# A fused attention and two mixture layers in one launch: a new hand-written order of all steps, and another buffer pair for two chunks

## The chip, the cores and the metric

The kernel runs on one core of a Trainium2 chip. The metric is the device time of one launch in microseconds (us). A core has TensorE for matmuls and transposes (PE in the profile, with its weight loads listed apart as PEld), VectorE (DVE), ScalarE (ACT), GpSimd (POOL), and SyncE (SP), which here only issues DMA transfers. Each engine runs its own instruction list in order; semaphores tie the lists together.

## The reference, cut to what matters

```
scores = q @ k.T / 8                         # 2 batches, 8 heads, 576 positions, 64 wide
scores[outside a window of 32] = -1e9        # heads 4 to 7: window of 128, every 4th key
attn   = softmax(scores);  x = attn @ v      # x: 1152 tokens x 512

h   = x @ w_in                               # 512 x 1024, w_in and w_out are float64
s   = h * softmax(h)
ln  = (s - mean(s)) / sqrt(var(s) + 1e-6) * g_ln
x   = ln @ w_out                             # 1024 x 512

p   = domain_probs / sum(domain_probs)
out = sum over 4 experts of p[:, e] * (relu(x @ w1[e]) @ w2[e])
```

All of it is float32 in accuracy: a matmul is made of three (hi x hi, hi x lo, lo x hi), so each operand is first split into a rounded hi and a lo = x - hi.

## The kernel before

**Attention** is cut into 12 units, UP.t.b and UD.t.b (P: plain heads, D: dilated heads; t = 0 to 2, b = batch). Each unit is a chain of steps, one instruction or a small group each: mask and scores on PE (L266, L275), max (L296), subtract (L298), exp (ACT L301), sum (L303), reciprocal (L305), normalise (L307), three PE transposes (L326) and a copy of them, product with v (PE L337), and the split of the result into `xhi` (L176) and `xlo` (L250). For five late units the transposes are done by a DVE block transpose and a bounce through DRAM (`da`, read back as `pt<-da`, L320).

**Weights.** `w_in` comes as float64 in four row blocks (`draw0` to `draw3`; block 0 in two halves, steps VI.0 and VI.4, the others VI.1 to VI.3) and is turned into hi and lo on the chip: low word and high word (ACT L190, L192), shift, or (DVE L194, L196), add (L198), hi (a cast, L176), lo (L225). `w_out` is converted likewise in the steps VO.j.t. The loads are lI.j and lO.j.t; lP, lD, lvp and lvd load the attention's operands, in place.

**First mixture layer.** H.t (t = 0 to 8, 128 tokens each) is x @ w_in (PE L367) in quarters or halves over the four row blocks of w_in; H.0:k and H.1:k below are quarter k, which needs the hi and lo of block k. Then come max, exp, s and a scaled difference. T.t transposes that into a buffer pair `hh`, `hl` that holds a chunk of three token tiles (chunk 0: T.0 to T.2, chunk 1: T.3 to T.5, chunk 2: T.6 to T.8); T.3 to T.8 go through DRAM (`dt`, `et`). X.c.dp is the product of chunk c with w_out (PE L444), copied into `xf`.

**Second mixture layer.** Each expert half g has an up product by Strassen's scheme, seven products of half the size (u.0 and u.1 for the two token halves, PE L568, with sums L585 to L617 on ACT, DVE and POOL), and a down product d.t (PE L640, summed into `xf` by L643 and L645). Its operands are prepared in small steps that add and split: WP.g for w1, WV.g for w2 (L483 loads it into `wl6`, `wl7`; a cast makes `wh4`, `wh5`; a subtraction makes the lo), XQ.s for x.

**Order.** A text table `ORDER` names 542 steps; the program walks through it and emits the next step of the named chain each time, so the table alone sets the order of instructions on every engine up to the first down products. A `+` behind a name changes the engine of that step where there is a choice: copies from ACT to DVE, `pick` from DVE to POOL, `poolv` from POOL to DVE. Steps F.n emit n warm-up matmuls (L86) whose results nobody reads. Behind the table a fixed loop emits the rest of the second layer, the same in both kernels.

**Buffers.** `hpools[0]` and `hpools[1]` hold one `hh`, `hl` pair each.

Of the kernel before, what the change touches and what calls it, by code (L numbers as in the profile page):

```python
# [30 lines left out]
ORDER = """
lP.0.0+ lI.4 VI.4+ F.1 F.3 UP.0.0 VI.4 UP.0.0+ F.4 lD.0.0 UP.0.0 VI.4 VI.4 UP.0.0 UD.0.0 UP.0.0+ VI.4+ lD.1.0+ UD.0.0 F.1 UD.0.0+ lP.1.0+ UP.0.0+ lI.0 lP.2.0
lD.2.0+ UD.1.0 UP.1.0 UD.1.0 UD.1.0+ VI.4 UD.0.0+ lI.1+ UP.1.0 UD.0.0 VI.0 lI.2+ UP.0.0+ UP.0.0 F.1 VI.0 UD.1.0+ UP.1.0+ VI.0+ lvp.0.0+ UP.0.0 VI.4+ F.10 VI.0
UD.1.0 UD.0.0 UP.2.0 UP.1.0+ UP.1.0+ UD.1.0+ UD.2.0+ UD.1.0 UP.2.0 VI.0+ UP.2.0+ UP.2.0 VI.1+ UD.0.0+ lvd.1.0+ VI.1+ VI.0+ VI.2+ VI.0+ VI.2 UP.1.0+ lI.3 UD.2.0
lvp.1.0 UD.1.0 UP.2.0+ UD.2.0 UP.1.0 UD.1.0+ UD.0.0 UD.2.0 F.3 VI.1+ UP.0.0 VI.1 UP.2.0+ UP.0.0 VI.1 UP.0.0+ UD.0.0 VI.2 VI.1 F.3 lvd.0.0 UP.1.0 UD.1.0+ UP.1.0
lD.1.1+ UD.1.0 UP.2.0+ VI.1 H.0+ VI.3 UP.1.0 lO.0.0+ misc+ VI.2+ UP.1.0 UD.1.0+ UD.1.1 VI.3+ lO.0.1 lD.0.1+ UD.2.0+ UP.1.0 VO.0.0 UD.1.1 lvd.2.0+ VI.3 VI.2+
UD.1.1+ UD.0.0+ VI.3 lvp.0.1 lP.0.1 lvd.2.1 UD.1.1 H.1 VI.2 UD.2.0 UD.0.0 VI.3 lD.2.1 UD.0.0 VO.0.1 VI.2 UD.2.0+ UD.1.1 VI.3 H.0+ H.1 UD.2.0 UD.1.1 lvp.2.0+
UD.0.1 UD.2.0 VO.0.1+ UP.0.1 VI.3+ UD.0.1 UP.0.1 lP.2.1 UD.0.1+ UP.0.1+ H.0 H.0 UP.2.0 VO.0.0 VO.0.0 UD.2.0 VO.0.1+ UD.0.1 lP.1.1+ UP.2.0 VO.0.0 VO.0.0+ VO.0.1+
UD.2.0 H.0+ UD.2.0 H.0+ UP.2.1+ VO.0.1+ lO.1.1+ UP.2.1+ UD.1.1+ endE+ VO.0.1+ UD.0.1+ H.1 UP.0.1+ UP.2.1+ lvd.0.1+ lvd.1.1 H.1 VO.0.1+ UD.0.1+ H.0 UD.2.1
UD.2.1+ H.1+ UP.2.0 H.2 UP.0.1 VO.1.1+ UD.0.1+ UP.0.1 UD.0.1+ VO.0.0+ UP.2.0 UD.2.1 H.1+ VO.0.0+ VO.1.1 lO.1.0+ H.2+ VO.1.1+ VO.1.1+ UD.2.1+ H.0+ UP.0.1+ UP.2.1  # L40
UP.0.1 UP.0.1 UP.2.0 UP.2.1 UP.1.1+ VO.1.0+ UD.2.1+ UD.0.1 VO.1.1+ H.1+ VO.1.1+ UD.1.1+ lO.2.1+ T.0 UP.1.1+ UD.2.1+ VO.1.0 T.0+ VO.1.0+ UP.1.1 H.3+ H.2+ UD.1.1
T.0 UD.0.1+ UP.0.1 H.3+ VO.1.0 UP.2.1+ VO.1.0+ T.0+ H.2+ UP.1.1+ UD.1.1 UD.2.1+ UD.0.1 H.2 UP.1.1 H.1+ UP.0.1 VO.2.1+ H.2+ UP.0.1+ UD.1.1 UD.2.1+ lO.2.0+ UD.0.1
UP.1.1 H.3+ VO.2.0 UD.1.1 VO.1.0 UP.2.1+ VO.1.1 UD.0.1+ VO.2.1+ UD.1.1 UD.2.1+ VO.1.0+ H.4+ H.3 T.1+ VO.2.1+ UP.2.1 VO.2.1+ lvp.1.1+ H.3+ VO.2.0 T.1+ T.2 T.1
VO.2.0+ H.5+ VO.2.0+ UD.2.1+ UP.2.1 T.2 T.2 H.4 H.5+ UP.1.1+ lvp.2.1+ UP.1.1+ T.1+ VO.2.0+ H.4 lO.3.0 UD.2.1+ T.2 VO.2.0+ UP.1.1+ H.4 VO.2.1 VO.2.1+ VO.3.0
UP.2.1 UD.2.1 VO.2.0 VO.3.0+ lO.3.1 H.5+ H.5+ UD.2.1 X.0.1+ VO.2.1+ UP.1.1+ VO.3.0 H.4+ VO.3.1 H.5+ VO.3.1 H.5+ H.3 UP.2.1 UP.1.1+ X.0.0 VO.3.0+ UP.1.1 VO.3.1+
VO.3.0 endA VO.3.1 UP.2.1+ T.3+ T.3+ VO.3.1+ VO.3.0 VO.3.1 VO.3.0+ VO.3.1 T.4 T.4+ X.0.1+ X.0.1 UP.1.1 UP.2.1+ T.3+ T.3+ X.0.0+ T.5+ X.0.0+ H.6+ T.4 T.3 H.6+
T.3 T.5+ T.5 H.8 T.4+ H.6 T.5+ T.4 H.6+ H.6 T.6 H.7+ H.8 T.6 H.8 T.4+ H.8+ T.5 H.8+ T.8+ H.7 H.7 T.6 T.6 H.7 T.5+ T.8+ T.6 H.7 X.1.0 X.1.0+ X.1.1 T.7+ T.7+ T.7+
T.8+ T.6+ X.1.0 T.8+ X.1.1+ sc endH T.8 X.1.1 T.7 XQ.0 XQ.0+ T.8 T.7+ T.7 X.2.0 XQ.0+ XQ.0 lW.0 XQ.0+ WP.0+ WP.0 XQ.0 WP.0 X.2.0 XQ.0+ WP.0 XQ.0 WP.0+ WP.0+
WP.0 WP.0 WP.0+ XQ.0+ XQ.0 X.2.1+ WP.0 XQ.0 WP.0+ WP.0+ WP.0 XQ.0 WP.0 XQ.0 XQ.0+ XQ.1 u.0+ XQ.0+ X.2.1 WP.0 u.0 lV.0+ endX XQ.1 XQ.1 u.0+ XQ.0 XQ.1 u.0 WV.0
XQ.1 WP.0+ u.0 u.0+ u.0 XQ.1 WP.0 u.0 u.0 lW.1 WP.0 u.0 u.0+ XQ.1 lW.2 WV.0 XQ.1 WV.0 WP.1+ u.1+ u.1 u.0 u.0+ u.0 u.0 u.0 WV.0 XQ.1+ u.0 u.0+ u.0 u.0+ u.0+ u.0  # L50
u.1+ u.0+ u.1 u.1+ XQ.1+ u.0+ u.1 u.1+ u.1 d.0 u.1+ XQ.1+ d.0+ WP.1 u.1 d.3+ XQ.1+ WP.1 d.3 XQ.1 XQ.1+ d.1+ WP.1+ WP.1 d.1 u.1+ u.1+ d.2 WP.1+ lV.1 WP.1 u.1+
u.1+ u.1 WP.1 WP.1 WP.1 u.1+ XQ.1 WP.1 d.2 WP.1 WP.1 u.1 XQ.1+ u.1 u.1 u.1+ WP.1+ WP.1 u.1 WP.1+ u.1 u.1+ u.1 WP.1 WP.1+
"""
# [758 lines left out]
```

## Time and profile before

| | |
|---|---|
| time, three runs | 525.57, 527.25, 528.87 us (median 527.25) |
| the profiled execution's own time | 526.15 us |
| its span in the trace | 524.4 us (1.75 us lie around it) |
| PE busy | 511.9 us, 98% of the span |
| DVE, ACT, POOL busy | 353.0, 191.5, 195.2 us |
| moved by DMA | 46.44 MB, 39.34 MB of it read |

The trace is one execution, 1.1 us below the median of the runs. A row of a timeline gives start, duration, engine, line, operation, the output and input tiles, and in brackets how long the engine had been idle before and what released it. Matmul rows are joined where they follow each other; a matmul's end is modelled, so rows overlap a little.

### The profile page before, as it was taken

The numbers are of one execution on the slowest core, as the hardware profiler recorded it, in microseconds if no ns is written. First come the engines' busy times: TensorE is split into PE (matmuls) and PEld (weight loads), VectorE is DVE, ScalarE is ACT, GpSimd is POOL, SyncE is SP. The second block draws the span as 40 slices with busy tenths as digits, with TensorE's granted clock in tenths as the row PEclk, the third lists the DMA queues.
The fourth block names the chain that finished last, engine by engine and source line by source line (L and its number), as shares of the span: only waits on it lengthen the run. The fifth ranks groups of instructions, "written<-read, shape, count | busy, mean of one in ns | idle before, by whom it ended". The sixth has DMA issues, their size and how long they took to land.

```text
span 524.4 us, 9407 instructions
## 1 busy us (share of the span) xinstructions
PE 511.9 (98%) x3966; PEld 457.8 (87%) x3971; DVE 353.0 (67%) x468; ACT 191.5 (37%) x296; POOL 195.2 (37%) x135
## 2 busy tenths in 40 slices
...
GB/s 326 406 322 159 178 158 71 153 162 201 53 202 67 1 1 87 75 1 1 160 1 1 40 121 0 1 161 1 2 0 162 1 0 81 0 1 1 1 81 100
DMA packets 24490, 46.44 MB, mean 89 GB/s; under 512 B 4480, under 2 KB 9088, under 8 KB 24064
## 3 DMA queue, kind: packets, MB, share of 16 engines
...
HBM read 39.34 MB, written 6.49 MB: 87 GB/s over the span
## 4 chain that ended last, share of the span: by engine, by line
PE 90%; DVE 4%; ACT 3%; DMA 2%; issue 1%; SPq 0%; DVEq 0%; ACTq 0%
PE pa L640 19%; PE pm L640 18%; PE pm L568 17%; PE pa L568 16%; PE pm L367 9%; PE pm L444 8%; PE pa L337 2%; DMA draw<-in_moe_w_in_dram 1%; DMA pt<-da 1%; DVE hl L487 1%; DVE xol L487 1%; ACT draw L190 1%; ACT cva L192 0%; DVE sw L487 0%; PE pa L275 0%
## 5 line engine op out<-in xcount | busy, mean ns | idle before, releaser
L581 DVE SCALAR_TENSOR_TENSOR hl<-ct,hh 128x512 fp32r<-128x512 f32 (+1 forms) x64 | 63.4, 1009 | 33.9 <-ACT hh L579 33.9
L579 ACT ACTIVATE hh<-ct 128x512 fp32r<-128x512 f32 (+1 forms) x64 | 42.1, 682 | 51.9 <-DVE ct L611 20.4
L640 PE MATMUL pa<-wl,hh 128*128 128x512 f32 (+1 forms) x148 | 57.2, 387 | 0.0
L640 PE MATMUL pa<-wh,hh 128*128 128x512 f32 (+1 forms) x148 | 57.2, 387 | 0.0
L640 PE MATMUL pa<-wh,hl 128*128 128x512 f32 (+1 forms) x148 | 57.1, 386 | 0.0
L640 PE MATMUL pm<-wl,hh 128*128 128x512 f32 (+1 forms) x144 | 55.7, 387 | 0.0
L640 PE MATMUL pm<-wh,hh 128*128 128x512 f32 (+1 forms) x144 | 55.7, 387 | 0.0
L640 PE MATMUL pm<-wh,hl 128*128 128x512 f32 (+1 forms) x144 | 55.6, 386 | 0.0
L487 POOL TENSOR_TENSOR wl<-wl,wh 128x1024 fp32r<-128x1024 f32 x7 | 16.9, 2413 | 95.6 <-ACT wh L176 95.6
L487 POOL TENSOR_TENSOR hl<-sw,hh 128x512 fp32r<-128x512 f32 x22 | 32.2, 1466 | 38.0 <-ACT hh L176 34.3
L645 DVE SCALAR_TENSOR_TENSOR xf<-pm,pr,xf 128x512 f32<-128x512 f32 (+1 forms) x32 | 23.6, 738 | 31.1 <-PE pm L640 31.1
L645 DVE SCALAR_TENSOR_TENSOR xf<-pa,pr,xf 128x512 f32<-128x512 f32 (+1 forms) x32 | 23.6, 738 | 30.3 <-PE pa L640 30.3
L176 ACT CAST wh<-wl 128x1024 fp32r<-128x1024 f32 x16 | 16.9, 1053 | 71.0 <-PE pa L640 40.6
L595 POOL TENSOR_TENSOR ct<-ct,ct 128x512 f32<-128x512 f32 (+1 forms) x15 | 21.8, 1454 | 44.5 <-ACT ct L593 40.7
L568 PE MATMUL pm<-xoh,hh 128*128 128x256 f32 (+1 forms) x192 | 33.4, 296 | 0.8 <-DVE ct L589 0.8
L568 PE MATMUL pa<-xoh,hl 128*128 128x256 f32 (+1 forms) x192 | 33.4, 296 | 0.0
L568 PE MATMUL pm<-xol,hh 128*128 128x256 f32 (+1 forms) x192 | 33.4, 296 | 0.0
L568 PE MATMUL pm<-xoh,hl 128*128 128x256 f32 (+1 forms) x192 | 33.4, 296 | 0.0
L568 PE MATMUL pa<-xol,hh 128*128 128x256 f32 (+1 forms) x192 | 33.4, 296 | 0.0
L568 PE MATMUL pa<-xoh,hh 128*128 128x256 f32 (+1 forms) x192 | 33.4, 296 | 0.0
L640 PEld LDWEIGHTS pa<-wh,hl 128*128 128x128 f32 x148 | 27.8, 188 | 5.6
L640 PEld LDWEIGHTS pa<-wh,hh 128*128 128x128 f32 x148 | 27.8, 188 | 5.4
...
## 6 DMA issues: line engine op xcount, KB each, us to landing
wl<-in_moe_w_dram SPq DMA_DIRECT2D x16, 512.0 KB, 4.4
cvr<-in_moe_w_out_dram SPq DMA_DIRECT2D x8, 512.0 KB, 5.4
rw<-in_moe_w_dram SPq DMA_DIRECT2D x8, 512.0 KB, 4.6
wh<-in_moe_w_dram SPq DMA_DIRECT2D x8, 512.0 KB, 6.5
...
dt<-st SPq DMA_DIRECT2D x5, 512.0 KB, 3.1
...
```

Of the source, the lines that this page charges most:

```text
L176: nc.scalar.copy(out, in_)
L190: nc.scalar.activation(out=low, in_=low.bitcast(U32), func=AF.Copy, scale=2.0 ** -29)
L337: nc.tensor.matmul(po[64 * (g % 2):64 * (g % 2) + 64, j, o:o + 32], lhsT=vt[rows, m, g, :], rhs=pt[rows, m, g, :], start=True, stop=True)
L367: nc.tensor.matmul(pm[:, n, :], lhsT=xx[:, kk, cols], rhs=ww["in", kk][:, 512 * n:512 * n + 512], start=(n_ == 0 and i < 2), stop=(n_ == K ...
L444: nc.tensor.matmul(pm[:, dd, 0:CW], lhsT=w_[:, o:o + 128], rhs=(ll if part == 2 else lh)[:, f, :], start=(f == 0 and part == 0), stop=(f = ...
L487: pick().tensor_tensor(out=out, in0=a, in1=b, op=op)
L568: nc.tensor.matmul(ps[:, ff, 0:n], lhsT=a[:, kk, fc], rhs=b[:, kk, :], start=kk == 0 and m == 0, stop=kk == 1 and m == 2)
L579: nc.scalar.activation(out=hv, in_=src, func=AF.Relu)
L581: nc.vector.scalar_tensor_tensor(out=lv, in0=src, scalar=0.0, in1=hv.bitcast(F32), op0=ALU.max, op1=ALU.subtract)
L595: poolv().tensor_tensor(out=c12, in0=c21, in1=c22, op=ALU.add)
L640: nc.tensor.matmul(po[:, 0, 0:dn], lhsT=h_[:, f, cols], rhs=w_, start=(f == 0 and i == 0), stop=(f == 3 and i == 2))
L645: nc.vector.scalar_tensor_tensor(out=acc[:, t, dc], in0=po[:, 0, 0:dn], scalar=pr[:, t, e:e + 1], in1=acc[:, t, dc], op0=ALU.mult, op1=ALU ...
```

## The change: a new table, and chunk 0 and 2 in one pair

The table `ORDER` is replaced as a whole; it names the same steps as often as before, among them 26 warm-up matmuls. On the engines' sides some `+` marks differ: small copies and subtractions move between ACT, DVE and POOL.

Chunks 0 and 2 now both use the pair in `hpools[0]`, chunk 1 has `hpools[1]` (before: chunks 0 and 1 shared pair 0, chunk 2 had pair 1). The first weights of the second layer, `prep_w1`, then lie in pair 1 and no longer in pair 0, and the up product's output buffers `hb` are made in `end_X` from a new pool (first token half) and on chunk 2's pair (second token half).

```diff
 ORDER = """
-lP.0.0+ lI.4 VI.4+ F.1 F.3 UP.0.0 VI.4 UP.0.0+ F.4 lD.0.0 ...
...
+lP.0.0+ lI.4 UP.0.0 VI.4+ F.3 lD.0.0 UP.0.0+ F.4 lD.1.0+ ...
...
@@ moe_T
-            p = hpools[c // 2]
+            p = hpools[c % 2]
@@ prep_w1
-            t6 = [hpools[0].tile([128, 6, 2, 256], F32R, name=n, tag=n) for n in ("hh", "hl")]
+            t6 = [hpools[1].tile([128, 6, 2, 256], F32R, name=n, tag=n) for n in ("hh", "hl")]
@@
-    hp1 = ExitStack()
+    sp1 = ExitStack()
@@ end_att
-        hpools[1] = hp1.enter_context(tc.tile_pool(name="hp1", bufs=1, side="right"))
-        spo[0] = hp1.enter_context(tc.tile_pool(name="spo", bufs=1, side="right"))
+        hpools[1] = ctx.enter_context(tc.tile_pool(name="hp1", bufs=1, side="right"))
+        spo[0] = sp1.enter_context(tc.tile_pool(name="spo", bufs=1, side="right"))
@@ end_X
-        hp1.close()
+        sp1.close()
         hp = ctx.enter_context(tc.tile_pool(name="hp", bufs=1, side="right"))
-        for i, n in enumerate((512, 640)):
-            hb.append([hp.tile([128, 4, n], F32R, name=f"h{x}{i}", tag=f"h{x}{i}") for x in "hl"])
+        hb.append([hp.tile([128, 4, 512], F32R, name=f"h{x}0", tag=f"h{x}0") for x in "hl"])
+        hb.append([hpools[0].tile([128, 4, 640], F32R, name=f"h{x}", tag=f"h{x}") for x in "hl"])
```

PE at the first product with w_in, in the order of before. `wh_168` is block 0 of w_in, `wh_411` block 1; `pt,vp` and `pt,vd` are products with v, and the first three rows are H.0:0.

```order
L367 MATMUL pm<-wh_168,xhi 128x512 x2
L367 MATMUL pm<-wl_169,xhi 128x512 x2
L367 MATMUL pm<-wh_168,xlo 128x512 x2
L337 MATMUL pa<-pt,vp 64x32 x24
L266 LDWEIGHTS identb
L266 MATMUL pa<-mask,identb 128x192
L266 LDWEIGHTS identb
L266 MATMUL pa<-mask,identb 128x192
L275 MATMUL pa<-qkD_123 32x64 x24
L337 MATMUL pa<-pt,vd_116 64x32 x24
```

The same place after; block 0 is `wh_195`, block 1 `wh_415`.

```order
L367 MATMUL pm<-wh_195,xhi 128x512 x2
L367 MATMUL pm<-wl_196,xhi 128x512 x2
L367 MATMUL pm<-wh_195,xlo 128x512 x2
L337 MATMUL pa<-pt,vp 64x32 x24
L367 MATMUL pm<-wh_415,xhi 128x512 x2
L367 MATMUL pm<-wl_416,xhi 128x512 x2
L367 MATMUL pm<-wh_415,xlo 128x512 x2
L326 MATMUL pa<-ident,pd_129 128x128 x3
L86 LDWEIGHTS warm
L86 MATMUL pm<-warm 128x512
```

H.0:1 has moved ahead of the scores of UD.1.1 and the product of UD.0.0, directly behind the product of UP.1.0.

DVE over the same stretch before: `eva_413` is block 1 of w_in under conversion, `cva_164` block 2, `wl1_412` the lo of block 1, `xlo_91<-pa_449` the lo of UP.0.0.

```order
L174 COPY pt_438<-pa_431 128x384
L194 TENSOR_SCALAR eva_413<-eva_413 128x1024
L196 SCALAR_TENSOR_TENSOR eva_413<-draw1_312,eva_413 128x1024
L305 RECIPROCAL st_406<-st_406 128x6
L198 ISA eva_413<-draw1_312,eva_413 128x2048
L250 TENSOR_TENSOR xlo_91<-pa_449,xhi_90 128x2x192
L194 TENSOR_SCALAR cva_164<-cva_164 128x1024
L225 TENSOR_TENSOR wl1_412<-eva_413,wh1_411 128x1024
L196 SCALAR_TENSOR_TENSOR cva_164<-draw2_318,cva_164 128x1024
```

And after (`xlo_91<-pa_444` is the lo of UP.0.0, `wl1_416` the lo of block 1):

```order
L194 TENSOR_SCALAR eva_417<-eva_417 128x1024
L305 RECIPROCAL st_410<-st_410 128x6
L196 SCALAR_TENSOR_TENSOR eva_417<-draw1_281,eva_417 128x1024
L250 TENSOR_TENSOR xlo_91<-pa_444,xhi_90 128x2x192
L198 ISA eva_417<-draw1_281,eva_417 128x2048
L194 TENSOR_SCALAR cva_164<-cva_164 128x1024
L196 SCALAR_TENSOR_TENSOR cva_164<-draw2_315,cva_164 128x1024
L225 TENSOR_TENSOR wl1_416<-eva_417,wh1_415 128x1024
```

The lo of UP.0.0 has moved ahead of the add (ISA) of block 1, and the "or" of block 2 ahead of the lo of block 1.

ACT where the second layer begins, before: `xf_1435<-pm_1860` is the copy out of X.2.1, `ct0_1923<-pa_1927` the copy of the first up product of u.0, `wh4_1975<-wl6_1944` the first cast of w2.

```order
L176 COPY xf_1435<-pm_1860 128x2x384
L176 CAST hh_1837<-sw3_1844 128x512
L585 COPY ct0_1923<-pa_1927 128x2x256
L176 CAST xoh_1765<-xf_1435 128x4x320
L176 CAST wh4_1975<-wl6_1944 128x1024
```

And after:

```order
L176 CAST wh4_1938<-wl6_1921 128x1024
L176 COPY xf_1415<-pm_1854 128x2x384
L176 CAST hh_1784<-sw3_1791 128x512
L585 COPY ct0_1904<-pa_1908 128x2x256
L176 CAST xoh_1705<-ct3_1710 128x2x256
L176 CAST xoh_1705<-xf_1415 128x4x320
```

The cast of w2 has moved ahead of the copy out of X.2.1 and of all that follows it.

At PE's start the four warm-ups that stood ahead of the first scores (UP.0.0) now stand behind them, so that seven and no longer four lie between the scores of UP.0.0 and those of UD.0.0; the number stays 26.

## Rows read from the trace of the kernel before

**Rows 1.** What PE waited for: us in total, times, longest.

```profile
PE pa L337 <- DMA pt<-da: 0.8, 1, 0.8
PE pm L568 <- DVE ct L589: 0.8, 1, 0.8
```

**Rows 2.** Busy time of each engine by stretch.

```profile
core 0: us, PE busy (x) PEld busy (x) DVE busy (x) ACT busy (x) POOL busy (x), PEclk, DMA share, GB/s
13.11:26.22 13.11, 9.11 (x252) 6.15 (x253) 13.01 (x25) 9.26 (x14) 5.71 (x5) 1.00 1.02 406
...
23.46:38.65 15.19, 14.20 (x295) 11.15 (x289) 14.18 (x24) 10.12 (x16) 7.18 (x4) 1.00 0.91 349
...
38.65:62.40 23.75, 22.86 (x462) 18.32 (x461) 22.47 (x42) 18.32 (x30) 10.06 (x10) 1.00 0.52 167
62.40:144.40 82.00, 82.00 (x575) 76.43 (x570) 60.48 (x85) 39.94 (x62) 21.15 (x12) 1.00 0.46 134
...
165.00:520.00 355.00, 355.00 (x2071) 321.84 (x2071) 216.16 (x246) 98.65 (x152) 135.65 (x85) 1.00 0.12 39
```

**Rows 3.** PE's timeline, the start and the first H product.

```profile
1.45 1.89 PE L86 MATMUL pm<-warm 128*128 128x512 bf16 x4 [1.45 <-DVE warm L81]
...
7.44 0.72 PE L275 MATMUL pa<-qkD 64*32 64x64 f32 x48 [0.36 <-DMA qkD<-in_qkd_dram]
...
11.21 2.11 PE L86 MATMUL pm<-warm 128*128 128x512 bf16 x9
...
19.88 0.90 PE L337 MATMUL pa<-pt,vp 64*64 64x32 f32 x48 [0.58 <-DMA vp<-in_vp_dram]
...
23.46 0.72 PE L367 MATMUL pm<-wh,xhi 128*128 128x512 f32 x2
...
25.05 0.76 PE L337 MATMUL pa<-pt,vp 64*64 64x32 f32 x35
...
37.32 0.62 PE L367 MATMUL pm<-wl,xhi 128*128 128x512 f32 x2
```

**Rows 4.** ACT, DVE and POOL, timelines before H.0's products.

```profile
21.27 0.45 ACT L176 CAST xhi<-pa 128x384 fp32r<-128x384 f32 x1
...
22.03 0.55 DVE L250 TENSOR_TENSOR xlo<-pa,xhi 128x384 fp32r<-128x384 f32 x1
...
23.26 1.21 DVE L225 TENSOR_TENSOR wl<-eva,wh 128x1024 fp32r<-128x1024 f32 x1
24.40 1.21 DVE L196 SCALAR_TENSOR_TENSOR cva<-draw,cva 128x1024 uint32<-128x1024 uint32 x1
...
31.16 1.67 POOL L307 TENSOR_TENSOR pd<-sm,st 128x384 f32<-128x384 f32 x1 [2.92 <-DVE st L305]
33.49 2.82 POOL L225 TENSOR_TENSOR wl<-eva,wh 128x1024 fp32r<-128x1024 f32 x1 [0.66 <-ACT wh L176]
```

**Rows 5.** ACT, SP and DVE, timelines at the change to the second layer.

```profile
144.59 0.80 ACT L176 COPY xf<-pm 128x768 f32<-128x768 f32 x1 [4.56 <-PE pm L444]
...
146.02 0.59 ACT L585 COPY ct<-pa 128x512 f32<-128x512 f32 x1
146.50 1.26 ACT L176 CAST xoh<-xf 128x1280 fp32r<-128x1280 f32 x1
147.66 1.06 ACT L176 CAST wh<-wl 128x1024 fp32r<-128x1024 f32 x1
...
140.43 1.75 SPq L483 DMA_DIRECT2D wl<-in_moe_w_dram  x2
...
148.84 1.48 DVE L487 TENSOR_TENSOR xol<-xf,xoh 128x1280 fp32r<-128x1280 f32 x1
150.24 0.68 DVE L589 TENSOR_TENSOR ct<-pm,ct 128x512 f32<-128x512 f32 x1
```

**Rows 6.** The page: loads of w2 and w1, KB each and us to landing.

```profile
wl<-in_moe_w_dram SPq DMA_DIRECT2D x16, 512.0 KB, 4.4
...
wh<-in_moe_w_dram SPq DMA_DIRECT2D x8, 512.0 KB, 6.5
```

More of the change, by code (lines that the diff above doesn't have):

```diff
@@ L31 @@
 ORDER = """
[L32 to L51, printed above, removed]
@@ L52 @@
-u.1+ u.1 WP.1 WP.1 WP.1 u.1+ XQ.1 WP.1 d.2 WP.1 WP.1 u.1 XQ.1+ u.1 u.1 u.1+ WP.1+ WP.1 u.1 WP.1+ u.1 u.1+ u.1 WP.1 WP.1+
+lP.0.0+ lI.4 UP.0.0 VI.4+ F.3 lD.0.0 UP.0.0+ F.4 lD.1.0+ UD.0.0 UP.0.0 F.1 VI.4 lP.1.0+ UP.0.0 UD.1.0 VI.4 lI.0 VI.4 lP.2.0 UP.0.0+ UD.0.0 UD.0.0+ UP.0.0+
+lD.2.0+ UD.1.0 UD.0.0+ lI.1+ UP.0.0+ VI.4+ UP.1.0 VI.0 UD.0.0 UD.1.0+ lI.2+ UD.0.0 lvp.0.0+ UP.1.0 UP.1.0+ F.3 UD.0.0 lvd.1.0+ VI.0 UP.0.0 UD.1.0+ F.10 UP.1.0+
+VI.0+ UD.2.0+ lI.3 UD.1.0 VI.4 VI.0 UD.1.0+ VI.0 UD.1.0+ UP.0.0 UP.2.0 UD.2.0 lvp.1.0 VI.0 VI.1+ F.3 UD.2.0 UD.1.0 UP.1.0+ UP.2.0 UP.2.0+ VI.4+ UD.1.0+ UD.0.0
@@ new lines @@
+UD.2.0 UP.1.0+ VI.1+ VI.2+ UP.0.0 UD.2.0+ UD.0.0 VI.1+ UP.0.0 UD.2.0 F.1 VI.0+ VI.1 UP.1.0+ lvd.0.0 UP.0.0+ VI.1 VI.2 UP.1.0 UD.1.0+ VI.1 lD.1.1+ UP.1.0 VI.2
+lO.0.0+ VI.2+ VI.3 UD.1.0 H.0+ VI.1 lO.0.1 UP.1.0 UP.2.0 H.0+ UP.1.0 UD.2.0+ UD.1.0+ UP.1.0 UP.2.0+ lD.0.1+ lvd.2.0+ VI.2+ UD.2.0 lvp.0.1 F.1 UD.1.1 VI.3+
+VO.0.0 UD.2.0 UD.0.0+ VI.3 VI.2 H.1 UP.2.0+ lP.0.1 lvd.2.1 VI.3 UP.2.0+ H.1 UD.0.0 UD.1.1 VI.2+ VO.0.1 VI.3 UD.1.1+ lD.2.1 UD.0.0 UD.1.1 UD.0.1 UP.0.1 VI.3
+lvp.2.0+ UD.1.1 UD.0.1 VO.0.1+ UP.0.1 UD.0.1+ UP.0.1+ H.0 lP.2.1 UD.0.1 UP.2.0 VI.3+ UD.0.1+ UD.1.1 VO.0.1+ H.0 VO.0.0 UP.2.0+ UP.0.1+ VO.0.1+ UD.2.0 UP.2.1+
@@ new lines @@
+UD.2.0 lP.1.1+ UD.1.1+ misc+ H.0+ VO.0.1+ UD.2.0 UP.2.1+ H.0+ lO.1.1+ H.0 VO.0.0 UD.0.1+ lvd.0.1+ UP.2.1+ UP.0.1 H.1 VO.0.0 H.1 UD.0.1 VO.0.0+ endE+ VO.0.1+
+UD.2.1 UD.2.1+ UP.2.0 UP.0.1 VO.1.1+ UD.2.1 UD.0.1+ VO.0.0+ UP.2.1 H.1+ UP.2.0 H.1+ VO.0.1+ UP.0.1 UP.2.1 H.2 UP.2.0 UP.2.1+ VO.0.0+ UD.0.1 H.0+ H.2+ H.1+
+lvd.1.1 UD.2.1+ UP.0.1 lO.1.0+ UP.1.1+ UP.1.1+ UP.0.1 UD.1.1+ VO.1.1 VO.1.1+ UD.1.1 UP.1.1 VO.1.1+ VO.1.1+ T.0 UP.2.1+ UD.0.1+ T.0+ T.0 VO.1.0+ H.2+ H.3+
+UD.2.1+ UD.2.1+ H.2+ VO.1.1+ UP.0.1 H.3+ UP.0.1 UD.2.1+ T.0+ UD.0.1 UD.1.1 UD.2.1+ VO.1.0 UP.0.1+ UD.2.1+ H.2 lO.2.1+ UP.1.1+ VO.1.0+ UD.1.1 VO.1.0 H.2+ H.3+
@@ new lines @@
+UD.1.1 UP.1.1 UD.0.1 UD.1.1 H.1+ H.3 UD.0.1+ UP.1.1 VO.1.0+ VO.1.1 UP.2.1 VO.2.1+ H.3+ VO.1.0 lO.2.0+ VO.2.1+ VO.2.0 VO.1.0+ H.4+ UD.2.1+ H.4 lvp.1.1+ T.1+
+UP.2.1 VO.2.0 T.1+ T.2 lvp.2.1+ VO.2.0+ VO.2.1+ T.1 H.4 T.2 T.2 VO.2.0+ UP.1.1+ UP.1.1+ UP.2.1 VO.2.0+ H.5+ UP.1.1+ T.1+ VO.2.1+ lO.3.0 VO.2.1+ VO.2.1+ H.4 T.2
+H.5+ UD.2.1+ VO.2.0+ H.3 lO.3.1 VO.3.0 UD.2.1 H.5+ VO.2.0 UP.2.1 H.5+ UP.1.1+ VO.3.1 VO.3.0+ VO.2.1+ VO.3.1 UD.2.1 H.5+ VO.3.0 X.0.1+ VO.3.1+ H.4+ VO.3.0+
+VO.3.1 VO.3.0+ H.5+ UP.1.1+ UP.1.1+ VO.3.0 UP.2.1 endA X.0.0 T.3+ VO.3.0+ VO.3.1+ T.3+ VO.3.1 VO.3.1 X.0.1+ T.4 T.4+ UP.2.1+ T.3+ X.0.1 T.3+ T.3 UP.1.1 X.0.0+
```

6 lines of the change are left out of this document (added).

## The prediction

> **What bounds the kernel now.** I read the busy times first, in the table above: PE is busy 98% of the span, and no other engine comes near. So a change of order can only take PE's idle time, or add to it, unless the matmuls change, and they don't: every row of a matmul that the old order has stands in the new one, and no tile gets another shape.
>
> Then the stretches, to see where the idle time lies [rows 2]. From 165 to 520 us PE is busy 355.00 of 355.00 us, from 62.4 to 144.4 us 82.00 of 82.00. Idle time is found at the start (9.11 busy of 13.11 us between 13.11 and 26.22, so 4.0 idle), 0.99 us between 23.46 and 38.65 (14.20 of 15.19), 0.89 between 38.65 and 62.4, and one gap at the change to the second layer. The list of waits names the two late ones [rows 1]: 0.8 us on a transposed attention tile coming back from DRAM (`pt<-da`), and 0.8 us for a sum on DVE (`ct`, L589).
>
> Why is PE idle at the start? Two things are full there [rows 2]: DVE with 13.01 of 13.11 us, and the DMA engines with a share of 1.02 at 406 GB/s. The operands must arrive, and DVE must convert w_in and do the softmaxes. That start ends where H.0's products fill PE; the first begins at 23.46 us [rows 3].
>
> **The change part by part.** I sum on the profiled execution, 526.15 us, and add 1.1 us for the distance to the median of the runs.
>
> *The buffers: 0.* Before, chunks 0 and 1 shared a pair, so chunk 1's copies waited for X.0's last reads and chunk 2's for nobody. Now chunk 2's copies wait for X.0, which is long done by then, and chunk 1's for nobody. That wait costs PE nothing now: 82.00 of 82.00 us busy from 62.4 to 144.4 holds all of X.0 and the copies of chunks 1 and 2 [rows 2]. H.6 to H.8, which need no chunk, cover it. `prep_w1` lies on chunk 1's pair in both kernels and waits for X.1's reads in both; the second half of `hb` lies on chunk 2's pair and waits for X.2, as its place did before. If the cover were gone, PE would wait for the tail of a chunk, a cast and a subtraction, some 2 us by the sizes of [rows 5].
>
> *The start of PE: late scores.* Three more warm-ups stand ahead of UD.0.0's scores. The first four take 1.89 us, 0.47 each; the nine at 11.21 take 2.11, 0.23 each [rows 3]. Three are thus 0.7 to 1.4 us. They cover the 0.36 us for which these scores wait for data now [rows 3], so the scores come 0.35 to 1.05 us later, and with them the DVE work that depends on them. DVE is full there, so I hand this delay on to what DVE does next.
>
> The four and the nine show TensorE's clock at its two levels: 1.2 GHz right after the idle start, 2.4 GHz at 11.21, after PE had worked with short breaks since 1.45; the granted clock stands at 1.00 in each stretch shown from 13.11 on [rows 2, 3]. The Trainium skill, "TensorE: Matmul & The Clock Gate", section "What's actually happening", says that the throttled state is the default and that activity releases it. By that rule, taking the four warm-ups from ahead of the first scores lets PE start where the four end now, at 3.34 and not 1.45 [rows 3], and the clock rise up to 1.9 us later; that activity comes ahead of the faster level, this one start shows. The forecast keeps the durations as they are; the later rise is a rival below.
>
> *H.0 begins earlier, H.0:1 meets a later lo.* On DVE the lo of UP.0.0 now stands ahead of the add (ISA) of block 1, an instruction over as many elements as the lo of block 1. H.0 can't start before UP.0.0's product (19.88 + 0.90 = 20.78, held by the arrival of vp [rows 3]), then its hi (0.45) and its lo (0.55 [rows 4]) and hand-offs: about 21.9, so 1.56 us earlier at best. But H.0:1 is moved directly behind UP.1.0's product and needs the lo of block 1, and ahead of that lo DVE now has the "or" of block 2, 1.21 us [rows 4], less some 0.4 us of small steps of the softmaxes that have moved behind (an estimate: less than one xlo of 0.55 [rows 4]). Before, that lo ended at 23.26 + 1.21 = 24.47. Now: + 0.8, + 0.35 to 1.05 from the late scores, so 25.6 to 26.3. The hi product of H.0:1 can go first, a third of the 1.59 us from 23.46 to 25.05 [rows 3], so H.0:1 starts at 25.1 to 25.8. In the old row of work it could have started behind UP.1.0's product, 25.05 + 0.90 = 25.95 [rows 3]. So the net gain is 0.15 to 0.85 us, whatever H.0:0 gains; I take 0.5, the middle. The best end, with a lo that isn't late at all and no idle time left: 1.56 + 0.99 = 2.55 us.
>
> *H.0:3 meets a later lo too.* Block 3's lo is on POOL, 33.49 to 36.31, and was needed at 37.32 [rows 3, 4]: 1.0 us to spare. In the new order block 2's lo, which DVE did, stands ahead of it on POOL. POOL had begun its last piece ahead of it (the normalisation) at 31.16 and ended it at 32.83 [rows 4]; one more lo of 2.82 gives 35.65, the next 38.5, 1.2 us too late. If POOL's earlier pieces are done sooner, nothing is late; if they are as late as the DVE's, 1.6. So 0 to 1.6 us, and I take 0.8.
>
> Sum to 38.65: -0.5 + 0.8 = **+0.3** (-2.55 to +1.45).
>
> *38.65 to 62.4: -0.5.* 0.89 us are idle. The new order sends the write of UD.1.1's and UD.2.1's bounces earlier and takes the read of UP.2.1 out from behind a w_out load on SP's queue, so the 0.8 us wait for `pt<-da` [rows 1] should shrink. But UP.2.1's product is moved ahead of a half of X.0, which then no longer covers the bounce of that unit, only that of UP.1.1. Ends: all of the 0.89 goes, or one more wait like the present one, +0.8. I take somewhat over half of the gain.
>
> *The change to the second layer: 0.* ACT's cast of w2 now stands ahead of X.2.1's copy and of u.0's first copy. It reads `wl6`, whose load is issued at 140.43 [rows 5] and takes 4.4 us as a median [rows 6]: 144.8. Cast 1.06, copy out 0.80, a small cast (some 0.6, as the copy), copy 0.59: u.0's copy ends at 147.9 where it ended at 146.6 (146.02 + 0.59 [rows 5]). The sum on DVE that PE waits for started at 150.24 [rows 5], since DVE had other splits in front; in the new order those stand behind it and it can run at about 148.7. So the wait of 0.8 us goes. What is late next is the same splits: u.1's first product needs XQ.1's lo, whose hi on ACT (1.26 [rows 5]) now starts behind u.0's copy and another cast, 148.5 to 149.8, and the lo on DVE (1.48 [rows 5]) is done at 151.3 to 152, where PE could go on with it from about 150.8: a wait of 0.5 to 1.2. -0.8 + 0.8 = 0. Ends: -0.8, if the split keeps pace; and if the load takes 6.5 us as the w1 loads do [rows 6], 2.1 us more in this chain, +2.0.
>
> *Behind 165 us: 0*, the code is the same and PE has no idle time [rows 2].
>
> **Sum:** 0.3 - 0.5 + 0 = -0.2 us. 526.15 - 0.2 = 525.95, plus 1.1 = 527.05: **527.0 us**, no change. The ends: -2.55 - 0.89 - 0.8 = -4.2 and +1.5 + 0.8 + 2.0 = +4.3. About 1%, 5.3 us, is what a measurement of this kernel can tell from no change; neither end reaches it.
>
> **The rivals.**
>
> *The order does what an order can (faster within 1%).* H.0 is 1.6 us earlier and nothing waits, the two late gaps close: up to -4.2, some 523 us. For it speaks that all these gaps have a named cause in the trace; against it that DVE and the loads are full at the start, so each earlier step has made another later. Chance 0.25. To be faster by over 1%, more idle time would have to go than the places that the change touches have; only the 4.0 us of 13.11 to 26.22 could give that: 0.05.
>
> *The start gets slower.* PE begins 1.9 us later (1.45 + 1.89 = 3.34 [rows 3]) and TensorE's clock rises 1.9 us later. Scores and warm-ups in that time run at half the rate, 0.95 us lost, on top of the 1.05 of the late scores; DVE, full, hands on the whole: +2.0, and with block 3's lo late (+1.6) 3.6: 527.2 + 3.6 = 531 us. It decides from the point where DVE has no idle time between UD.0.0's scores and H.0, and it had 0.1 us [rows 2]. Against it: warm-ups fill PE there and PE's idle time is 4.0 us. Chance 0.2 for this or the next, within 1%; over 1% only both together (3.6 + 2.0 = 5.6, 533 us), with what no row prices: 0.10.
>
> *ACT blocks the second layer.* The load lands after 6.5 us: +2.0, 529 us; two such waits (the second cast stands in the same order, further back) 531.
>
> *The buffers matter after all.* If a wait for X.0's reads is hidden in the trace by an engine that has slack, freeing it changes no time: that is the forecast. A gain would need PE to wait there, and it doesn't.
>
> **How the numbers follow.** No change around the forecast, within 2 us, 0.40; faster within 1% 0.25; faster over 1% 0.05; slower within 1% 0.20; slower over 1% 0.10. Faster by over 1%: 0.05, within 1% 0.85, slower by over 1% 0.10. The range reaches from 523.5 (most of the good end) to 531.0 (the slow start, or two blocked casts).
>
> **What would show it.** In the new trace: PE's first scores at the same time as before, UD.0.0's scores 0.35 to 1.05 us later; H.0's first product between 21.9 and 23.5; a wait ahead of H.0:1 or H.0:3 for DVE's or POOL's L225; less wait for `pt<-da`; at the second layer ACT idle on the landing of `wl`, no wait for L589 and one for L487; and the same 355 us behind. I am wrong if PE's idle time before 62 us differs by more than 3 us, or if new waits show between 62 and 144 us.

## The result and the profile after

The changed kernel takes 529.96 us (median of 8 runs, 527.92 to 530.76); the kernel before, run with it, 525.89 us (median of 8, 525.06 to 528.87). The ratio is 1.0063 (95% interval 1.0047 to 1.008): slower by 4.1 us or 0.6%. The time lies inside the forecast range, but no change was forecast, and the interval leaves no room for none: the prediction was wrong. The profiled execution took 530.46 us, its span is 528.7 us, 4.3 more than before.

The stretches of the changed kernel, to be held against [rows 2]:

```profile
core 0: us, PE busy (x) PEld busy (x) DVE busy (x) ACT busy (x) POOL busy (x), PEclk, DMA share, GB/s
...
13.11:26.22 13.11, 9.51 (x220) 6.85 (x220) 12.15 (x23) 9.99 (x16) 6.14 (x5) 0.87 1.02 409
23.46:38.65 15.19, 14.48 (x240) 11.15 (x245) 12.30 (x15) 8.97 (x15) 7.27 (x3) 0.68 0.93 357
...
38.65:62.40 23.75, 23.68 (x470) 18.76 (x462) 22.86 (x45) 15.88 (x27) 8.94 (x7) 1.00 0.31 105
62.40:144.40 82.00, 80.55 (x643) 73.76 (x642) 60.53 (x85) 46.51 (x73) 23.31 (x15) 1.00 0.48 143
...
165.00:520.00 355.00, 355.00 (x2068) 321.83 (x2067) 218.12 (x252) 99.15 (x152) 136.36 (x86) 1.00 0.11 38
```

The column to look at is PEclk. Before it was 1.00 in every stretch of [rows 2]; now it is 0.87 and 0.68 around H.0's first products. PE is not idle there: from 23.46 to 38.65 us it is busy for 14.48 us, before for 14.20, and it does less. A busy time says nothing of the rate. Cut finer, the fall has two edges:

```profile
20.00:22.88 2.88, 1.43 (x51) 1.24 (x52) 2.21 (x4) 1.92 (x4) 1.76 (x2) 1.00 0.99 401
22.88:33.12 10.24, 9.72 (x113) 7.64 (x114) 8.25 (x12) 6.83 (x12) 4.59 (x2) 0.50 1.03 401
33.12:38.65 5.53, 5.04 (x129) 3.79 (x135) 4.64 (x4) 2.73 (x5) 2.68 (x2) 1.00 0.74 280
```

For 10.24 us TensorE ran at 1.2 and not 2.4 GHz. PE's timeline across the first edge, to be held against [rows 3]:

```profile
16.86 0.59 PE L86 MATMUL pm<-warm 128*128 128x512 bf16 x2 [0.16 <-issue]
17.30 0.49 PE L326 MATMUL pa<-ident,pd 128*128 128x128 f32 x3
18.70 0.52 PE L326 MATMUL pa<-ident,pd 128*128 128x128 f32 x3 [0.92 <-DVE sm L298]
20.64 0.92 PE L337 MATMUL pa<-pt,vp 64*64 64x32 f32 x48 [1.41 <-DVE eva L194]
22.30 0.52 PE L326 MATMUL pa<-ident,pd 128*128 128x128 f32 x3 [0.74 <-ACT pt L176]
23.18 1.50 PE L337 MATMUL pa<-pt,vd 64*64 64x32 f32 x48 [0.36 <-DVE xlo L250]
24.61 1.22 PE L367 MATMUL pm<-wh,xhi 128*128 128x512 f32 x2
25.63 1.05 PE L367 MATMUL pm<-wl,xhi 128*128 128x512 f32 x2
...
40.09 0.73 PE L367 MATMUL pm<-wh,xhi 128*128 128x512 f32 x2
```

And before, the warm-ups on either side of the product of UP.0.0 (19.88 in [rows 3]; of each three that are emitted the trace has two) and the start of H.0's third quarter:

```profile
18.13 0.52 PE L326 MATMUL pa<-ident,pd 128*128 128x128 f32 x3 [1.28 <-DVE sm L298]
18.70 0.59 PE L86 MATMUL pm<-warm 128*128 128x512 bf16 x2
...
20.93 0.59 PE L86 MATMUL pm<-warm 128*128 128x512 bf16 x2 [0.16 <-issue]
22.15 0.55 PE L326 MATMUL pa<-ident,pd 128*128 128x128 f32 x3 [0.62 <-ACT pt L176]
...
35.37 0.73 PE L367 MATMUL pm<-wh,xhi 128*128 128x512 f32 x2
```

Ahead of the fall PE did two groups of transposes, a product with v and a third group in somewhat over 5 us, with waits of 0.9, 1.4 and 0.7 us between. The product of UD.1.0 takes 1.50 us where such a product took 0.90, H.0's pairs 1.22 and 1.05 where they took 0.72 and some 0.6 [rows 3]. H.0 begins 1.15 us late; H.0's third quarter, at 35.37 before, begins at 40.09, 4.7 late. Below, "the distance" is this: how much later PE begins the same product in the new trace than in the old one.

Behind that, in the order of time: the wait for `pt<-da` [rows 1] is gone (the distance falls from 4.5 to 3.5 us); a new wait stands ahead of X.1, and behind it the distance is 5.3:

```profile
PE pm L444 <- DVE e L381: 1.3, 1, 1.3
```

The wait for L589 is gone (distance 4.35), in the way that was summed: ACT's cast starts when the load lands, the copy of u.0 comes behind it, and DVE's sum runs at 152.86 with no gap on PE behind it. The rows answer to [rows 5]:

```profile
149.51 1.06 ACT L176 CAST wh<-wl 128x1024 fp32r<-128x1024 f32 x1 [6.06 <-DMA wl<-in_moe_w_dram]
150.47 0.79 ACT L176 COPY xf<-pm 128x768 f32<-128x768 f32 x1
...
151.68 0.59 ACT L585 COPY ct<-pa 128x512 f32<-128x512 f32 x1
...
152.86 0.69 DVE L589 TENSOR_TENSOR ct<-pm,ct 128x512 f32<-128x512 f32 x1
```

From 165 to 520 us PE is full as before, and the distance stays 4.35 us to the last matmul.

Times of single executions spread with the clock: each run comes with a mean granted clock, and 10 us at 1.2 GHz make it 0.990. Of 156 runs of the kernel before, in five sittings, 20 have 0.990 or less (median 527.97 us) and 99 have 0.996 or more (525.37). Of the changed kernel's 8 runs, 4 have 0.990 or less (530.6) and two have 0.996 or more (528.2). So the fall of the clock costs about 2.5 us where it comes, it comes oftener in the changed kernel, and some 2.8 us of loss stand beside it (by those two runs). The runs whose clock did not fall at all say the same: with a mean clock of 1.00 the changed kernel took 528.5 us once and f4 below, its order with the warm-ups placed otherwise, 527.6 to 529.3 in three runs, where the old order with the new buffers (e4) took 524.6 to 525.6 in six. No trace of the changed order at that clock was kept.

### The profile page after: what moved, and what is told of

Same layout as the page of the kernel before. It is cut to its first block, busy times and chain, and to the rows that moved or that the text cites. A ratio compares the mean times of both kernels' runs of the same rounds, so it can differ in the third digit from the quotient of the medians.

```text
span 528.7 us, 9407 instructions
## 1 busy us (share of the span) xinstructions
PE 515.3 (97%) x3965; PEld 460.5 (87%) x3971; DVE 354.2 (67%) x466; ACT 192.7 (36%) x297; POOL 197.8 (37%) x136
## 4 chain that ended last, share of the span: by engine, by line
PE 82%; DMA 6%; DVE 4%; ACT 3%; issue 2%; SPq 1%; DVEq 0%; ACTq 0%
PE pa L640 19%; PE pm L640 18%; PE pm L568 17%; PE pa L568 17%; PE pm L444 6%; PE pm L367 3%; DMA draw<-in_moe_w_in_dram 2%; DMA et<-dt 2%; DMA dt<-st 1%; PE pa L337 1%; DMA cvr<-in_moe_w_out_dram 1%; PE pa L275 1%; ACT e L374 1%; SPq L151 1%; ACT xhi L176 1%
## 5 line engine op out<-in xcount | busy, mean ns | idle before, releaser
L579 ACT ACTIVATE hh<-ct 128x512 fp32r<-128x512 f32 (+1 forms) x64 | 42.3, 682 | 60.1 <-DVE ct L611 26.1
L176 ACT CAST wh<-wl 128x1024 fp32r<-128x1024 f32 x16 | 16.9, 1054 | 76.1 <-PE pa L640 39.6
L487 POOL TENSOR_TENSOR hl<-sw,hh 128x512 fp32r<-128x512 f32 x20 | 29.9, 1497 | 29.5 <-ACT hh L176 24.0
```

The lines of the kernel that those rows point to most:

```text
L487: pick().tensor_tensor(out=out, in0=a, in1=b, op=op)
L579: nc.scalar.activation(out=hv, in_=src, func=AF.Relu)
```

## The experiments

All were timed in five rounds beside the kernel before (its medians: 525.7 to 526.1). "Low" counts runs with a mean clock of 0.990 or less; "high" is the median of the runs at 0.996 or more, with their number. Of the theories in the expectations, A is the fall of the clock and B the late first scores; both are told in full in that of e1. An interval here is that of the ratio to the kernel before; where two intervals overlap, the difference between two medians is not told from nothing with certainty.

| run | median us | ratio to before, 95% | low | high |
|---|---|---|---|---|
| changed kernel | 529.96 | 1.0047 to 1.008 | 4 of 8 | 528.2 (2) |
| e1_fill | 529.57 | 1.0027 to 1.0085 | 0 of 12 | 529.1 (10) |
| e2_start | 529.09 | 1.0021 to 1.0074 | 5 of 12 | 528.1 (2) |
| e3_old_begin | 526.44 | 0.9972 to 1.0035 | 3 of 12 | 526.1 (9) |
| e4_buffers | 525.21 | 0.9953 to 1.0012 | 2 of 12 | 525.1 (9) |
| e5_old_12us | 529.51 | 1.0039 to 1.0084 | 4 of 7 | 528.0 (1) |
| e6_old_25us | 528.22 | 1.0015 to 1.0057 | 2 of 12 | 527.5 (7) |
| e7_lo_on_dve | 528.44 | 1.0036 to 1.0074 | 3 of 10 | none |
| e8_new_tail | 524.6 | 0.9963 to 0.9995 | 2 of 12 | 524.5 (9) |
| e9_h01_back | 529.47 | 1.0017 to 1.0072 | 2 of 12 | 529.7 (3) |
| e10_h01_lo | 529.18 | 1.0015 to 1.0063 | 2 of 12 | 529.0 (1) |
| e11_exp_first | 529.47 | 1.0026 to 1.0079 | 3 of 12 | 528.2 (1) |
| e12_h01_alone | 527.61 | 0.9987 to 1.0045 | 4 of 12 | 525.8 (5) |
| f1_25us_h01 | 528.69 | 1.0 to 1.0057 | 2 of 12 | 528.4 (8) |
| f2_25us_lo | 528.31 | 0.9986 to 1.0039 | 2 of 12 | 527.8 (10) |
| f3_fewer_warm | 527.67 | 0.9985 to 1.0031 | 8 of 12 | none |
| f4_same_count | 529.39 | 1.0016 to 1.0068 | 0 of 12 | 529.4 (10) |
| h1_old_334 | 525.38 | 0.9974 to 1.0028 | 2 of 12 | 524.6 (7) |
| h2_more_warm | 526.63 | 1.0002 to 1.0032 | 0 of 12 | 526.3 (10) |

### Which part of the change: the buffers, the begin, the rest

**e4_buffers** puts the old table into the changed kernel.

> The old order with the new buffers only. Theories A and B: 0, within 0.3% of the kernel before (525.9). Rival D (the buffers cost time): the wait ahead of X.1 shows and the time is 1 to 4 us more.

525.21 us: the buffers cost nothing. Rival D falls.

**e3_old_begin** takes the first 156 steps, to H.0's end, in the old order and the other 386 as the new table has them. (The orders made from two tables below are made the same way.)

> The steps up to the end of H.0 (156 of 542) in the order of before, the rest in the new order, new buffers. If the whole loss lies ahead of 40 us (theories A and B alike): PE reaches 38.65 as before, then the 1.2 us gained at the bounce and the 1.0 us at the second layer stay and the wait of 1.3 us ahead of X.1 stays or not: 524 to 526. Rival C (the later order or the buffers lose the time): 528 to 530.

526.44 us: by the medians 3.5 of the 4.1 us lie ahead of 40 us, and the new order behind it loses 1.2 against e4. The intervals of e3 and e4 overlap, but e3's trace has 1.0 us of the wait ahead of X.1, and e4's has none.

**e2_start** puts four warm-ups back ahead of the first scores.

```diff
-lP.0.0+ lI.4 UP.0.0 VI.4+ F.3 lD.0.0 UP.0.0+ F.4 lD.1.0+ UD.0.0 UP.0.0 F.1 ...
+lP.0.0+ lI.4 F.1 F.3 UP.0.0 VI.4+ lD.0.0 UP.0.0+ F.4 lD.1.0+ UD.0.0 UP.0.0 ...
```

> The changed kernel with four warm-ups put back ahead of the first scores (26 in all, four and no longer seven between the scores of UP.0.0 and UD.0.0). Theory A: UD.0.0's max comes 1.1 us earlier, but PE is as idle between 17 and 23 us, so the clock still falls: 529. Theory B: H.0 begins at 23.5 and the time falls by 1.1 us or more; if the fall of the clock came from the lateness too, by 4, to 526.

529.09 us, 5 of 12 runs with a low clock. **e5_old_12us** takes the first 48 steps in the old order.

> The first 48 of 542 steps (PE's first 13 us, through the ten warm-ups) in the old order, the rest in the new order with the new buffers. Theory B' (the loss comes from the late scores of the first 10 us, which DVE hands on): as with the old order up to H.0, 526.4. Theory E (it is lost between 13 and 40 us, where H.0:1 follows at once and PE has fewer warm-ups between its small products): as the changed kernel, 529 to 530.

529.51 us. Theory B falls with both: neither the late first scores nor the clock's later rise make the loss. **e6_old_25us** takes 103 steps.

> The first 103 steps (through H.0:0 and UP.1.0's product, PE's first 26 us) in the old order, the rest new. Theory B': 526.4. Theory E: 526.4 if what is lost between 13 and 26 us (warm-ups, clock, order of DVE's conversions) makes it up, 528 or more if H.0:1 directly behind UP.1.0's product and block 2's lo on POOL do.

528.22 us, between the two: by the medians some 1.3 us belong to steps 49 to 103 and 1.8 to steps 104 to 156; the intervals of neighbours overlap, so the division is rough.

### The clock

**e1_fill** adds warm-ups where PE is idle ahead of the fall.

```diff
+F.3 ahead of UP.0.0's product with v
-F.1
+F.3 behind it
```

> The changed kernel with five more warm-up matmuls (31 and not 26): three ahead of UP.0.0's product with v, two more behind it, where PE was idle for 1.4 and 0.7 us. Theory A (the clock): TensorE's clock falls to 1.2 GHz at 22.9 us because PE did little just ahead of it; filled, the clock stays at 1.00 and the time falls by 2.5 to 3.5 us, to about 526.5. Theory B (the late start): everything runs 1.1 us late since the first scores, the clock is a side effect of a few per cent; the time stays at 529 to 530.

No run of twelve has a low clock any more, and yet the median is 529.57. **f4_same_count** does the same with 26 warm-ups in all (the ten at 12.6 us become five).

> The changed kernel with its 26 warm-ups placed otherwise: five of the ten at 12.6 us go to 19 to 22 us, three ahead of UP.0.0's product and two more behind it. Theory G: no run with a clock of 0.99 or less and 1 to 1.5 us less than the changed kernel, 528.5. Rival: no change, 529.5 to 530.

Again no low clock, and 529.39. So theory A, as I had it, falls: the long fall of the clock can be taken away without getting the time back. What stands in its place is seen on PE's timeline of f4:

```profile
25.59 0.77 PE L337 MATMUL pa<-pt,vp 64*64 64x32 f32 x36
28.14 0.42 PE L337 MATMUL pa<-pt,vp 64*64 64x32 f32 x12 [1.78 <-issue]
28.49 0.73 PE L367 MATMUL pm<-wh,xhi 128*128 128x512 f32 x2
```

PE stops for 1.78 us in the midst of one product of 48 matmuls, between two that wait for nothing. In the kernel before, the same product (25.05 in [rows 3]) has a gap of the same kind, less than half as long:

```profile
26.55 0.42 PE L337 MATMUL pa<-pt,vp 64*64 64x32 f32 x13 [0.75 <-issue]
```

"issue" means that the profile shows no semaphore that ended it. In f4 the clock then falls for a shorter time, behind this gap:

```profile
26.00:29.79 3.79, 2.01 (x42) 1.64 (x35) 2.67 (x5) 2.85 (x6) 3.18 (x1) 1.00 1.02 396
29.79:33.20 3.41, 3.41 (x80) 2.40 (x82) 2.83 (x6) 2.34 (x4) 2.11 (x2) 0.50 1.03 395
```

**f3_fewer_warm** asks the reverse, in the order of e8 (below), whose begin is the old one: the three warm-ups ahead of UP.0.0's product are left out, and of the three behind it two.

```diff
-F.3 ahead of UP.0.0's product with v
-F.3
+F.1 behind it
```

> The best order so far (old up to X.1, then new: 524.6) with five warm-ups fewer between 18 and 22 us: none ahead of UP.0.0's product and one behind it, as in the changed kernel; 21 in all, nothing else. Theory G (fewer warm-ups there let the clock fall for 10 us around H.0): a mean clock of 0.99 or less in most runs and 2 us more, 526.5. Rival (the fall comes from the lateness of the new order): 524.6, with the clock as often low as before.

527.67 us against 524.6, and 8 of 12 runs with a low clock against 2. Nothing else differs, and the five matmuls are read by nobody. So in the old order the warm-ups at this place keep the clock up in most executions, and they are worth 3.1 us by the medians. The two runs were timed in different sittings, and by the ratios to the kernel before (1.0008 and 0.9979, with intervals that overlap a little) it is 1.5 us. In f3's trace:

```profile
15.50:19.00 3.50, 1.62 (x56) 1.18 (x54) 3.47 (x10) 2.12 (x3) 2.20 (x2) 1.00 1.01 405
19.00:29.28 10.28, 9.23 (x157) 6.90 (x155) 8.57 (x13) 6.95 (x11) 4.09 (x2) 0.50 1.02 400
```

**h2_more_warm** goes on in the other direction from e8: five and not three at each of the two places.

> The best order so far (old up to X.1, then new: 524.6) with two warm-ups more at each of the two places between 18 and 22 us (30 in all). Theory G: the clock falls in fewer runs still (none at 0.99 or less), median 524.4 to 524.6, and the mean 0.3 us lower. Rival (more instructions of PE ahead of H.0 make it wait for its own instructions, as in e1): 525.5 to 526.

No low clock in twelve runs, but 526.63 us: 2 us more than e8. Here the intervals lie apart. Its trace has gaps like that of f4, but short ones of 0.2 and 0.3 us, and a wait of 1.2 us for a hi on ACT; one profile can't say what made the median. More of the same is not better.

### The moves between 26 and 40 us

**e12_h01_alone** moves H.0:1 directly behind UP.1.0's product in the old order, with the new buffers; **e9_h01_back** moves it back in the changed kernel.

> The old order with the new buffers and H.0:1 moved directly behind UP.1.0's product: this one move alone. Theory E1: 1 to 2 us more than the old order with the new buffers (525.2). Theory G: 0, since nothing changes ahead of 25 us; PE waits for the lo of block 1 at most 0.3 us.

> The changed kernel with H.0:1 back in its old place on PE, behind UD.0.0's product and H.1:0; nothing else. Theory E1 (H.0:1 directly behind UP.1.0's product makes PE wait for block 1's lo and for its own instructions while other work stands behind): 1 to 2 us less than the changed kernel, 528 to 528.5. Theory G (the fall of the clock at 23 us is the loss): the time stays at 529.5 to 530, for PE is as idle ahead of 23 us as in the changed kernel.

The move alone costs 2.4 us at the median (527.61 against e4's 525.21), 0.7 in the runs with a high clock; undone in the changed kernel it gives 0.5. The intervals overlap in both cases, so neither figure is told from nothing with certainty.

**e7_lo_on_dve** changes one mark (`VI.2+` to `VI.2`), so that block 2's lo is on DVE; **e10_h01_lo** does both.

> The changed kernel with the lo of w_in's block 2 on DVE as before and not on POOL. In the changed kernel's trace the add of block 3 on DVE takes 3.2 us beside that lo, where it takes 1.2 alone. Theory F (DVE held up by POOL makes block 3 late): the add takes 1.2 us and the time falls by 0.5 to 2 us. Theories B' and E: PE does not wait for block 3, within 0.5 us of the changed kernel.

> Both: H.0:1 in its old place and the lo of block 2 on DVE. If the two are separate losses of 1.5 us each: 526.5 to 527. If each only uncovers the other (one wait ends when the other does): 528 to 528.5, like the lo alone.

e7 is 1.5 us faster at the median, e10 0.8; the intervals of both overlap that of the changed kernel. That DVE was held up is seen in the changed kernel's trace, the add of block 3 and POOL's lo of block 2:

```profile
34.49 3.22 DVE L198 CUSTOM_DVE_ANT_0 eva<-draw,eva 128x2048 uint16<-128x2048 uint16 x1
...
34.23 2.40 POOL L225 TENSOR_TENSOR wl<-cva,wh 128x1024 fp32r<-128x1024 f32 x1 [0.83 <-ACT wh L176]
```

The same add took 1.21 us at 23.04, with POOL idle. **f1_25us_h01** and **f2_25us_lo** undo each in e6.

> As e6 (first 103 steps old, rest new) with H.0:1 back behind UD.0.0's product and H.1:0. If that move is what the new order loses between 26 and 40 us: 526.4, the time of the old order up to the end of H.0. If block 2's lo on POOL is: 528.2, as e6.

> As e6 with block 2's lo on DVE. The other half of the same question: 526.4 if the lo on POOL is what is lost between 26 and 40 us, 528.2 if not.

528.69 and 528.31: by the medians neither brings e6 (528.22) to e3 (526.44), but f2's interval can't be told from that of either. No single move of these is shown to be the loss between 26 and 40 us. In e6 and f2 the trace has the same sort of gap as in f4, a little further on:

```profile
33.87 0.39 PE L367 MATMUL pm<-wh,xhi 128*128 128x512 f32 x1 [1.50 <-issue]
```

(f2; 1.30 us at 34.19 in e6.) In e6 H.0's third quarter begins at 37.59, in e3 at 35.64: this gap is the larger part of those 1.95 us.

### The later part

**e11_exp_first** moves H.8's exp on ACT ahead of T.4's cast, on which the chain of the new wait ahead of X.1 hung.

```diff
-T.4 (cast) H.8 (exp)
+H.8 (exp) T.4 (cast)
```

> The changed kernel with H.8's exp on ACT ahead of T.4's cast; nothing else. In the changed kernel's trace PE waits 1.3 us ahead of X.1 for DVE's last read of H.8, which stands behind that exp, which stands behind the cast that waits for T.4's way through DRAM. Theory H (that queue order is the wait): the wait goes, 1.0 to 1.3 us less, 528.7. Rival (T.4's data is late for X.1 anyway): the wait stays with another name, no change.

529.47 us. The wait stays under another name, 1.7 us for the cast of T.4 itself (`PE pm L444 <- ACT hh L176`). The rival is right: T.4's data is late for X.1. It is late from its write to DRAM on: T.5's block transpose, which needs the buffer that is written out, waits 4.07 us for that write in the changed kernel, where the old order has 2.36 (the second row):

```profile
99.56 1.25 DVE L412 STREAM_TRANSPOSE st<-e 128x1024 f32<-128x1024 f32 x1 [4.07 <-DMA dt<-st]
...
93.84 1.25 DVE L412 STREAM_TRANSPOSE st<-e 128x1024 f32<-128x1024 f32 x1 [2.36 <-DMA dt<-st]
```

**h1_old_334** takes 334 steps in the old order, up to those transposes, **e8_new_tail** 400, to the end of X.1.

> The old order up to the first transposes that go through DRAM (334 steps), the rest new, new buffers. The old order up to H.0's end (156 steps) takes 526.4, up to X.1's end (400 steps) 524.6. If the new order's loss of the later part lies in the chain T.3, T.4, T.5, H.8 ahead of X.1: 526, with a wait of about 1 us ahead of X.1. If it lies between 40 and 88 us: 524.6 and no such wait.

> The old order up to the end of X.1 (400 steps), the rest new, new buffers. If the changed kernel's gain of 1.0 us at the second layer (no wait for L589 ahead of u.1) is real: 1.0 us less than the old order with the new buffers, about 524.2, and faster than the kernel before by 0.2 to 0.3%. If it came from the late begin (loads of w2 had more time), the gain goes: 525.2.

h1: 525.38 us, 524.6 in the runs with a high clock, so the second case: no wait ahead of X.1, and the transpose waits 2.39 us: the same steps T.3 to T.8 in the same new order don't lose time when what comes ahead of them, 40 to 88 us, is in the old order. What in that stretch makes the write late stays open. e8: 524.6 us, ratio 0.9979 (0.9963 to 0.9995), the fastest of all: the old order up to X.1, with the new order's second layer.

## Why the prediction was wrong

**The step that failed** is the sum to 38.65 us, +0.3 (-2.55 to +1.45); the distance at H.0's third quarter is +4.7, of which 1.15 stand when H.0 begins and some 3.6 come behind that, while the clock is down. Its working took every duration of PE from [rows 3] ("The forecast keeps the durations as they are") and asked only what waits for what. PE's rate was no constant: between the transposes of UD.0.0 and UP.1.0, around UP.0.0's product, the new order has one warm-up where the old one has six, the clock fell to 1.2 GHz at 22.9 us, and 9.7 us of PE work ran at half rate. I had counted the warm-ups (26 in both) and priced the three that moved at the very start, but not where the others had gone. f3 shows that in the old order the warm-ups at this place keep the clock up in most executions, and that without five of them it loses 1.5 to 3 us.

The runs with warm-ups put back (e1, f4) show that this is not all. Without the long fall, the new begin still loses as much. In these two traces PE then stands still 1.8 to 1.9 us in the midst of a product, where it was 0.75 us before, and the clock falls for 3.4 us behind that. So two things that the sum didn't have lie one behind the other, and taking away one uncovers the other. That this explains the 3 us which are lost in executions at a clock of 1.00 too is not shown. For the 1.8 us of the steps 104 to 156 no single move came out as the cause: neither H.0:1's place nor the lo on POOL, undone in two surroundings each, gave them back clear of the noise.

**H.0 earlier:** it came 1.15 us later. The product of UP.0.0 began at 20.64 and not 19.88 (the row names a DVE step that the product doesn't need; in e7 the same wait, 1.2 us, is on the arrival of vp), and the next product ran at half rate. The earlier lo of UP.0.0 on DVE had no way to show.

**H.0:1 and its lo:** the lo of block 1 came at 27.3 us, forecast 25.6 to 26.3; a wait doesn't show since PE at half rate came later still. One row was read wrongly here: 25.05 + 0.90 = 25.95 takes the product of UP.1.0 for whole, but the row of [rows 3] holds 35 of its 48 matmuls, and the other 13 come behind the gap of 0.75 us and end at 26.97. The gap that is so much longer in e1 and f4 could be seen in that trace. **H.0:3:** no wait either, for the same reason, though the lo on POOL ended at 42.2.

**The late scores** were sized right, at the upper end of 0.35 to 1.05: UD.0.0's max at 9.30 and not 8.20, +1.1 us. Handing them on was wrong: e5, with the first 48 steps in the old order, is as slow.

**38 to 62 us:** -0.5 forecast, about -1.05 in the trace. But e4, in the old order, has that gap closed too (PE busy 23.63 of 23.75 us), so the new order's queue on SP is not shown to be the reason.

**Buffers:** 0, right (e4). But "that wait costs PE nothing", 62.4 to 144.4 us full, held for the old order alone: in the new one PE has 1.45 us idle there, 1.3 of them the wait ahead of X.1, by another chain than the buffers'. That the stretch was full I took to mean slack; it had none to spare for T.4's way through DRAM.

**The second layer:** forecast 0 = -0.8 + 0.8; in the trace it gave -1.0, and e8's trace keeps it (PE busy 20.60 of 20.60 us from 144.4 to 165, in e4 19.82). By the medians e8 is 0.6 us ahead of e4, with intervals that overlap. The wait for L589 went by the mechanism that was told, and what I put in its place, u.1 waiting for XQ.1's lo, didn't come: that lo was done at 155.5 and PE is full from 144.4 to 165 us.

**What can be told apart:** the prediction took 1%, 5.3 us, for the least that a measurement can tell from no change. This one told 0.6%.

The rival that came nearest is "the start gets slower": its place and its engine were right, its mechanism wasn't (the later rise of the clock). The later rise did come: UD.0.0's scores at 8.29 us take 0.97 us in the changed kernel, where those at 7.44 took 0.72 before. But in e2 and e5 they take 0.72 again, at 7.64 and 7.82, and neither is faster clear of the noise.
